# A new order for the instructions of the experts' stage, from a search with another rule for shared waits of VectorE and GpSimd

## The chip, the cores and the metric

The kernel runs on one core of a Trainium2 chip. The metric is the device time of one execution in microseconds (us), taken as the median of several runs. Five engines work side by side, each through its own queue in the order in which the program issued the instructions: TensorE (PE in the profile, with its weight loads as PEld), VectorE (DVE), ScalarE (ACT), GpSimd (POOL) and SyncE (SP), which here only starts transfers. An instruction waits on semaphores for results of other engines; whatever stands behind it in the same queue waits too.

## The reference

Two stages. Attention with packed keys: for each of 8 batches and 8 heads, `p_packed = softmax(p k^T / 8) v` with 32 packed rows, and `out = softmax(q p_packed^T / 8) p_packed`. The result is read as 4608 tokens of 512 features. Then a mixture of 8 experts with a greedy assignment:

```python
cap = N // E                       # 576 tokens for each expert
order = np.argsort(-logits.flatten())
for idx in order:                  # best pairs (token, expert) first
    tok, e = idx // E, idx % E
    if assigned[tok] >= 0 or counts[e] >= cap: continue
    assigned[tok] = e; counts[e] += 1
for e in range(E):
    mask = assigned == e
    out[mask] = np.maximum(x[mask] @ w1[e], 0.0) @ w2[e]   # 512 -> 1024 -> 512
```

## The kernel before

Attention comes first, some 140 us, in an order of its own (`ORDER`), which the change leaves alone. The experts' stage follows. For each of the 8 experts, in the order in which they fill up, three strands run at once.

The matrix work of the expert whose turn it is: every factor is split into a high and a low part, and each product is three matmuls (high by high, high by low, low by high). The hidden layer has 8 slices. For slice f, token half m and product j, `f1.k.f.m.j` is a group of four matmuls (L1390); `h_hi` (ScalarE, L1396) takes the rectified high part out of PSUM and `h_lo` (VectorE, L1401) the low part, which frees the PSUM bank. `f2.k.f.t` multiplies a slice into the output tile t (L1410 to L1412, for t = 4 L1414 and L1415). The hidden tiles and the small products of the search share three PSUM banks. At an expert's end `ev` (ScalarE) and `ev_b` (VectorE, L1433) take the outputs out, and five `scatter` transfers on GpSimd's queue (L1446, indirect) write them to the tokens' rows.

The weights of the next experts: `load` (SyncE), then `split_h` (ScalarE, L1368) makes the high part and `split_l` (GpSimd, L1374) the low part, in four instructions of a quarter each. This is the splitting that the change speaks of.

The search for later experts' tokens, mostly on VectorE: `build_a` and `build_b` (L1065, L1066) with `build_v` set up the values, eleven rounds of `count_a` (ScalarE), `count_v` (VectorE, L1104), `count_m` (TensorE, L1110, L1111) and `upd_a/b/c` (VectorE) close in on a threshold, and `slot_a` to `slot_f`, `slot_v` (two instructions, L1263), `onehot` (L1267), `list_m` (TensorE) and `list_a/s/b` turn the chosen tokens into lists. `slot_e` is L1250 to L1252. Five `gather` transfers on GpSimd's queue (L1302, indirect) fetch the rows, `xg_st` and `xg_ld` store and reload them turned, and `xt_t` (L1317), `xs_h` and `xs_l` (L1329) make the two parts of the tokens' tile.

Nothing of this order is found at run time. `PACE` is one long list of names, `step.expert.…`, that an offline search wrote, and `Later.emit` issues the steps in that order, so that each engine's queue is that list with the other engines' steps left out:

```python
def emit(self):
    order = [tuple(int(i) if i.isdigit() else i for i in k.split('.')) for k in PACE.split()]
    for k in order:
        self.ops[k][2]()
```

Times such as `LEN` and `LAND` in the file fed the search; they are not used on the chip. Waits between engines are set from what the instructions read and write.

Of the kernel before, what the change touches and what calls it, by code (L numbers as in the profile page):

```python
# [1768 lines left out]
```

## Time and profile before

| what | us |
|---|---|
| median of 3 runs | 601.55 |
| the runs | 601.39 to 603.48 |
| the profiled execution, its own time | 600.76 |
| its span, first to last instruction | 599.0 |
| TensorE busy | 580.4 (97%) |
| VectorE busy | 399.0 (67%) |
| ScalarE busy | 341.8 (57%) |
| GpSimd busy | 369.1 (62%) |

The span is what the engines' rows cover; the rest of an execution's own time lies around it. Busy time of TensorE is the union of its matmuls' spans, and a matmul's span reaches into the next one's, so a busy share tells that the queue didn't run dry, not that every start came as early as it could. The granted clock of TensorE is 0.997 of full speed over the span.

### The profile page before, as it was taken

How to read it: one execution, taken by the hardware profiler on the slowest of the kernel's cores; microseconds unless marked ns; L12 is line 12 of the kernel's file. 1: busy time of each engine (PE TensorE's matmuls, PEld its weight loads, DVE VectorE, ACT ScalarE, POOL GpSimd, SP SyncE). 2: the span in 40 equal slices, each digit the busy share in tenths (PEclk: the TensorE clock that was granted, in tenths of full speed). 3: DMA queues.
4: the chain of work that ended last, by engine and by line, in shares of the span. 5: the costliest groups of instructions: out<-in, count | busy, mean ns of one | idle time of the engine just before them, and what ended most of it. 6: DMA issues, size and time to landing. Idle time of an engine off the chain costs nothing.

```text
span 599.0 us, 12421 instructions
## 1 busy us (share of the span) xinstructions
PE 580.4 (97%) x4145; PEld 494.3 (83%) x4145; DVE 399.0 (67%) x1438; ACT 341.8 (57%) x873; POOL 369.1 (62%) x617
## 2 busy tenths in 40 slices
...
GB/s 291 391 370 261 307 333 231 192 159 225 170 10 242 123 164 208 220 91 166 249 130 113 149 242 131 150 197 182 53 203 210 239 78 196 212 8 80 1 1 84
DMA packets 75307, 105.76 MB, mean 177 GB/s; under 512 B 7124, under 2 KB 54756, under 8 KB 75236
## 3 DMA queue, kind: packets, MB, share of 16 engines
...
q8 instruction: 35, 0.57, 0.4%
q10 hardware_dynamic: 576, 0.34, 0.2%
q14 instruction: 36, 0.29, 0.2%
...
## 4 chain that ended last, share of the span: by engine, by line
PE 87%; DVE 5%; ACT 2%; POOL 2%; issue 1%; DMA 1%; SPq 0%; POOLq 0%; DVEq 0%; ACTq 0%
PE hp L1390 34%; PE y L1410 10%; PE y L1411 10%; PE y L1412 9%; PE s L530 9%; PE xp L715 4%; PE y L1414 3%; PE y L1415 2%; PE pp L589 1%; DMA kl<-in_k_dram 1%; PE tr L574 1%; PE pl L1273 1%; PE px L1335 1%; ACT ja L1098 1%; POOL sb L653 1%
## 5 line engine op out<-in xcount | busy, mean ns | idle before, releaser
L1401 DVE SCALAR_TENSOR_TENSOR h<-hp,h 128x64 fp32r<-128x64 f32 (+3 forms) x192 | 61.8, 352 | 107.4 <-ACT h L1396 106.7
L1396 ACT ACTIVATE h<-hp 128x288 fp32r<-128x288 f32 (+2 forms) x128 | 51.7, 407 | 134.0 <-PE hp L1390 65.9
L1374 POOL TENSOR_TENSOR w1l<-w1s,w1h 128x256 fp32r<-128x256 f32 x124 | 89.7, 754 | 53.4 <-ACT w1h L1368 53.2
L1374 POOL TENSOR_TENSOR w2l<-w2s,w2h 128x256 fp32r<-128x256 f32 x124 | 90.5, 761 | 47.2 <-ACT w2h L1368 47.1
L1410 PE MATMUL y<-w2h,h 128*128 128x512 f32 x256 | 103.8, 406 | 0.0
L1411 PE MATMUL y<-w2l,h 128*128 128x512 f32 x256 | 100.6, 393 | 0.0
L1412 PE MATMUL y<-w2h,h 128*128 128x512 f32 x256 | 100.2, 391 | 0.0
L1390 PE MATMUL hp<-xh,w1h 128*128 128x288 f32 (+2 forms) x512 | 89.7, 298 | 1.0 <-DVE h L1401 0.9
L1390 PE MATMUL hp<-xh,w1l 128*128 128x288 f32 (+2 forms) x512 | 90.1, 299 | 0.0
L1390 PE MATMUL hp<-xl,w1h 128*128 128x288 f32 (+2 forms) x512 | 89.8, 298 | 0.0
L1390 PEld LDWEIGHTS hp<-xh,w1h 128*128 128x128 f32 x512 | 77.8, 188 | 7.4 <-ACT h L1396 1.1
L1446 POOL DMA_INDIRECT out_dram<-xg,gi x40 | 39.3, 983 | 69.7 <-DVE xg L1433 35.7
L1098 ACT ACTIVATE ja<-Vt,nT 128x288 bf16<-128x288 f32 x116 | 62.2, 536 | 32.7 <-DVE nT L1125 24.7
L1390 PEld LDWEIGHTS hp<-xl,w1h 128*128 128x128 f32 x512 | 76.4, 188 | 3.5 <-DVE xl L1346 0.2
L1390 PEld LDWEIGHTS hp<-xh,w1l 128*128 128x128 f32 x512 | 76.0, 188 | 2.9
L1412 PEld LDWEIGHTS y<-w2h,h 128*128 128x128 f32 x256 | 48.1, 188 | 10.8
L1302 POOL DMA_INDIRECT xg<-xd,gi x40 | 38.2, 955 | 23.1 <-issue 9.2
L1410 PEld LDWEIGHTS y<-w2h,h 128*128 128x128 f32 x256 | 48.1, 188 | 4.8
L1411 PEld LDWEIGHTS y<-w2l,h 128*128 128x128 f32 x256 | 48.2, 188 | 4.5
L1116 DVE SCALAR_TENSOR_TENSOR g<-pc,thr,s4r 128x3 f32<-128x3 f32 x64 | 14.0, 219 | 41.2 <-PE pc L1111 40.9
L1368 ACT CAST w2h<-w2s 128x1024 fp32r<-128x1024 f32 x32 | 33.3, 1042 | 13.1 <-DMA w2s<-in_moe_w_dram 6.7
L715 PE MATMUL xp<-P,th 128*128 128x264 f32 (+2 forms) x160 | 38.2, 328 | 0.7 <-DVE xs L742 0.3
...
## 6 DMA issues: line engine op xcount, KB each, us to landing
...
```

What stands on the lines that cost most here:

```text
L530: nc.tensor.matmul(t[:, 224 + 9 * a:224 + 9 * b], w[:, db].rearrange("p a b -> p (a b)"), x[:, :, db, a:b].rearrange("p b (t y) -> p t b y ...
L715: nc.tensor.matmul(xp[:m, :n], T[a, g][:, o:o + m], T[w, g][:, :n], start=i == 0, stop=i == 2)
L1098: nc.scalar.activation(ja, Vf, AF.Sign, bias=S_['nT'][:, j:j + 1], scale=-1.0, accum_out=cp[:, j:j + 1])
L1302: nc.gpsimd.indirect_dma_start(out=X['xg', k, c][:m], out_offset=None, in_=xd, in_offset=bass.IndirectOffsetOnAxis(ap=X['gi', k][:m, c:c + ...
L1374: eng.tensor_sub(X[n + 'l', k, q][r], X[n + 's', k, q][r], X[n + 'h', k, q][r].bitcast(F32))
L1390: nc.tensor.matmul(X['hp', k, f, n], X[W, k, q][:, d, 128 * r:128 * r + 128], X[Z, k][:, d, cut(k) * n:576 * n + cut(k) * (1 - n)], start= ...
L1396: nc.scalar.activation(X['h', k, f][:, cut(k) * n:576 * n + cut(k) * (1 - n)], X['hp', k, f, n], AF.Relu)
L1401: V.scalar_tensor_tensor(h[:, o:o + b - a], p[:, a - t * n:b - t * n], 0.0, h[:, a:b].bitcast(F32), op0=OP.max, op1=OP.subtract)
L1410: nc.tensor.matmul(y, hh, wh, start=f == 0, stop=False)
L1411: nc.tensor.matmul(y, hh, wl, start=False, stop=False)
L1412: nc.tensor.matmul(y, hl, wh, start=False, stop=f == 7)
L1446: s = nc.gpsimd.indirect_dma_start(out=out, out_offset=bass.IndirectOffsetOnAxis(ap=X['gi', k][:m, t:t + 1], axis=0), in_=X['yo', k, t][:m ...
```

## The change

Only the list `PACE` is changed, from the middle of the search for expert 2's tokens (behind the second gather for expert 1) to the first products of expert 5; further on, only a few exchanges of near neighbours are left. Every step stays, with the same instructions and the same data: no instruction is added or removed, and each engine does the same work in another order. 428 of TensorE's 852 steps, 344 of VectorE's 626, 164 of ScalarE's 343, 58 of GpSimd's 144 and 47 of SyncE's 118 stand at another place of their queue. The search that wrote the new list went on from the old one, with a model in which every VectorE instruction that is in flight when a splitting begins behind an indirect transfer waits until the whole splitting has ended. On GpSimd's queue, 20 splittings stand directly behind a gather or a scatter before, and 18 after. Cut to the lines that the text speaks of:

```diff
@@ -125,114 +125,113 @@
...
-    upd_c.2.3 build_k.2 f1.0.6.0.2 gather.1.1 split_h.1.1.2 f1.0.6.1.1 count_m.2.3 f2.0.4.1 upd_a.2.3 h_hi.0.6.0 split_l.1.1.1 upd_b.2.3 f2.0.5.3 upd_c.2.4 count_a.2.4 h_lo.0.6.0
-    f1.0.6.1.2 count_v.2.4 f1.0.7.0.0 h_hi.0.6.1 split_h.1.2.1 count_m.2.4 f1.0.7.0.1 h_lo.0.6.1 upd_a.2.4 f1.0.7.0.2 gather.1.2 upd_b.2.4 load.1.3.1 count_v.2.5 count_a.2.5 f2.0.5.1
...
-    scatter.1.3 xs_l.2.4 f2.1.7.1 slot_d.3 ev_b.1 f1.2.0.1.0 build_a.4 scatter.1.4 f1.2.0.1.1 f1.2.0.1.2 build_b.4 f2.1.6.0 split_l.2.3.2 h_hi.2.0.1 split_h.2.3.1 slot_e.3 f2.1.7.0
-    h_lo.2.0.1 build_t.4 ev.1.1 f1.2.1.0.2 build_v.4 ev.1.0 f1.2.1.1.0 build_s.4 count_v.4.0 h_hi.2.1.0 f1.2.1.1.1 count_a.4.0 slot_f.3 scatter.1.1 load.3.1.2 f1.2.1.1.2 slot_v.3
...
-    count_v.4.1 split_h.3.0.2 h_lo.2.1.1 f1.2.2.0.1 split_l.2.3.1 list_a.3 count_m.4.1 f1.2.2.0.2 upd_a.4.1 upd_b.4.1 f1.2.2.1.0 h_hi.2.2.0 count_a.4.2 list_s.3 f2.2.0.0 list_b.3
...
-    f2.2.7.3 ev.2.1 f2.2.7.4 xs_l.3.4 ev.2.3 f1.3.0.0.0 build_b.5 ev.2.4 scatter.2.3 f1.3.0.0.1 split_h.3.3.1 ev_b.2 f1.3.0.0.2 slot_b.4 f2.2.6.2 xs_l.3.5 scatter.2.1 h_hi.3.0.0
-    build_t.5 slot_c.4 build_v.5 f2.2.7.0 slot_d.4 split_l.3.3.2 slot_e.4 f1.3.0.1.0 h_lo.3.0.0 f2.2.7.2 build_s.5 count_v.5.0 count_a.5.0 f1.3.0.1.1 build_k.5 f1.3.0.1.2 ev.2.2
...
-    upd_a.5.1 split_l.3.3.1 upd_b.5.1 list_m.4 upd_c.5.2 count_a.5.2 f2.3.0.2 count_v.5.2 list_a.4 f2.3.0.0 h_hi.3.2.0 h_lo.3.2.0 count_m.5.2 list_s.4 f2.3.1.3 upd_a.5.2 upd_b.5.2
...
-    f2.3.3.3 h_hi.3.5.0 count_a.5.10 h_lo.3.5.0 f1.3.5.1.1 count_v.5.10 f1.3.5.1.2 split_h.4.2.2 f1.3.6.0.0 count_m.5.10 f2.3.4.1 upd_a.5.10 h_hi.3.5.1 upd_c.5.10 split_l.4.2.2
...
-    xs_l.4.1 slot_d.5 f1.3.7.1.0 split_h.4.3.1 build_s.6 split_l.4.3.2 xt_t.4.3 f2.3.6.1 slot_e.5 xs_h.4.3 f1.3.7.1.1 xt_t.4.4 f1.3.7.1.2 xs_l.4.3 build_t.6 f1.4.0.0.0 h_hi.3.7.1
-    h_lo.3.7.1 split_l.4.3.1 f2.3.6.2 build_v.6 xt_t.4.5 f2.3.6.4 count_a.6.0 f2.3.6.3 count_v.6.0 f2.3.7.4 xs_h.4.4 f2.3.7.1 xs_h.4.5 ev.3.4 load.5.1.1 xs_l.4.5 f2.3.7.0 split_h.5.0.1
...
-    f2.4.4.2 h_hi.4.6.0 split_h.5.3.1 h_lo.4.6.0 slot_a.6 f2.4.5.2 xs_l.5.1 xs_l.5.0 f2.4.4.3 split_l.5.3.1 slot_b.6 test_k.7 f1.4.7.0.0 xt_t.5.2 f2.4.5.4 xt_t.5.3 slot_c.6 xs_h.5.2
...
-    xs_h.5.4 split_l.5.2.2 slot_e.6 f1.4.7.1.1 slot_f.6 f1.5.0.0.0 xt_t.5.5 f1.5.0.0.1 f1.5.0.0.2 f1.4.7.1.2 h_hi.5.0.0 load.6.0.2 f2.4.6.4 h_lo.5.0.0 h_hi.4.7.1 f2.4.6.1 onehot.6
-    xs_h.5.5 load.6.0.1 split_h.5.3.2 slot_v.6 f1.5.1.0.0 f1.5.1.0.1 xs_l.5.5 split_l.5.3.2 load.6.1.1 f2.4.6.2 h_lo.4.7.1 xs_l.5.4 f1.5.1.0.2 list_m.6 member.7 f2.4.6.0 f1.5.0.1.0
...
+    upd_c.2.3 build_k.2 f1.0.6.0.2 gather.1.1 split_h.1.1.2 f1.0.6.1.1 count_m.2.3 f2.0.4.1 upd_a.2.3 h_hi.0.6.0 gather.1.2 upd_b.2.3 f2.0.5.3 upd_c.2.4 count_a.2.4 h_lo.0.6.0
+    f1.0.6.1.2 count_v.2.4 gather.1.3 f1.0.7.0.0 h_hi.0.6.1 count_m.2.4 f2.0.4.4 upd_a.2.4 split_l.1.1.1 upd_b.2.4 f1.0.7.0.1 upd_c.2.5 count_a.2.5 f1.0.7.0.2 h_lo.0.6.1 count_v.2.5
...
+    f1.2.0.1.0 slot_d.3 h_lo.2.0.0 f1.2.0.1.1 slot_e.3 ev.1.2 build_b.4 f1.2.0.1.2 scatter.1.2 f1.2.1.0.0 slot_f.3 h_hi.2.0.1 ev.1.3 f1.2.1.0.1 h_lo.2.0.1 split_h.3.0.1 onehot.3
+    build_t.4 f1.2.1.0.2 scatter.1.3 build_v.4 f1.2.1.1.0 h_hi.2.1.0 build_s.4 ev_b.1 f1.2.1.1.1 count_a.4.0 count_v.4.0 f1.2.1.1.2 scatter.1.4 h_lo.2.1.0 f2.2.0.2 h_hi.2.1.1 slot_v.3
+    count_m.4.0 f1.2.2.0.0 split_l.2.3.2 upd_a.4.0 h_lo.2.1.1 f1.2.2.0.1 upd_b.4.0 f1.2.2.0.2 list_m.3 h_hi.2.2.0 count_a.4.1 f1.2.2.1.0 h_lo.2.2.0 list_a.3 f1.2.2.1.1 upd_c.4.1
+    split_l.2.3.1 load.3.1.2 f1.2.2.1.2 count_v.4.1 list_s.3 h_hi.2.2.1 count_m.4.1 f2.2.0.1 upd_a.4.1 upd_b.4.1 list_b.3 f1.2.3.0.0 count_a.4.2 upd_c.4.2 f2.2.0.4 count_v.4.2
...
+    xs_h.3.2 h_lo.2.6.1 slot_a.4 f2.2.5.4 xs_l.3.2 f1.2.7.0.1 xs_l.3.1 f1.2.7.0.2 close_b.5 f1.2.7.1.0 h_hi.2.7.0 f1.2.7.1.1 h_lo.2.7.0 build_a.5 f2.2.6.1 f2.2.5.2 slot_b.4 build_b.5
+    split_h.3.3.2 f2.2.6.3 xt_t.3.3 build_t.5 slot_c.4 split_h.3.3.1 split_l.3.3.2 f1.2.7.1.2 build_s.5 build_v.5 f2.2.6.2 count_v.5.0 h_hi.2.7.1 xs_h.3.3 slot_d.4 f1.3.0.0.0
+    h_lo.2.7.1 count_a.5.0 xt_t.3.4 f2.2.6.0 f1.3.0.0.1 xs_l.3.3 load.4.1.2 f1.3.0.0.2 xt_t.3.5 f2.2.6.4 h_hi.3.0.0 count_m.5.0 xs_h.3.4 f2.2.7.4 upd_a.5.0 slot_e.4 xs_h.3.5 f2.2.7.3
...
+    list_a.4 f1.3.2.0.0 upd_b.5.2 upd_c.5.3 count_a.5.3 f1.3.2.0.1 count_v.5.3 split_l.3.3.1 f1.3.2.0.2 list_s.4 h_hi.3.2.0 f2.3.1.3 split_h.4.0.2 count_m.5.3 f2.3.0.4 upd_a.5.3
...
+    xs_h.4.2 split_h.4.3.1 build_a.6 slot_a.5 f2.3.5.3 split_h.4.2.2 f1.3.7.0.2 xs_l.4.2 f1.3.7.1.0 build_b.6 h_hi.3.7.0 split_l.4.2.2 f2.3.5.0 slot_b.5 build_s.6 h_lo.3.7.0 f1.3.7.1.1
+    xt_t.4.3 build_t.6 f1.4.0.0.0 build_v.6 xs_h.4.3 f1.3.7.1.2 xt_t.4.4 split_h.4.3.2 f2.3.6.0 xs_l.4.3 split_l.4.3.1 f1.4.0.0.1 h_hi.3.7.1 xs_h.4.4 h_lo.3.7.1 f2.3.6.1 count_a.6.0
+    count_v.6.0 f1.4.0.0.2 xt_t.4.5 f2.3.7.0 h_hi.4.0.0 xs_h.4.5 h_lo.4.0.0 split_l.4.3.2 count_m.6.0 slot_c.5 load.5.1.1 upd_a.6.0 f2.3.6.3 slot_d.5 upd_b.6.0 load.5.0.2 count_v.6.1
...
+    f1.4.6.1.0 xs_l.5.0 f1.4.6.1.1 xs_h.5.1 split_l.5.2.2 f1.4.7.0.0 xt_t.5.2 f1.4.7.0.1 xs_l.5.1 f1.4.6.1.2 f1.4.7.0.2 f2.4.5.3 h_hi.4.7.0 load.6.0.2 xs_h.5.2 h_lo.4.7.0 f2.4.5.4
...
+    h_hi.4.7.1 split_l.5.3.2 f1.5.1.0.1 h_lo.4.7.1 f2.4.6.2 xs_l.5.4 xs_l.5.5 f1.5.1.0.2 f2.4.6.4 member.7 list_m.6 split_l.5.3.1 f2.4.6.0 load.6.1.2 f1.5.0.1.0 h_hi.5.1.0
```

## Rows read from the trace of the kernel before

**Rows 1.** stretches of the run: span, its length, busy us (instructions) by engine, clock, DMA
```profile
196.00:266.00 70.00, 70.00 (x454) 59.67 (x453) 51.24 (x250) 46.66 (x117) 43.76 (x63) 1.00 0.53 159
266.00:276.00 10.00, 9.02 (x55) 7.60 (x55) 9.58 (x26) 5.63 (x13) 8.72 (x13) 1.00 0.61 197
276.00:320.00 44.00, 44.00 (x284) 38.36 (x284) 31.71 (x146) 25.66 (x65) 25.21 (x34) 1.00 0.60 174
320.00:336.00 16.00, 15.16 (x110) 13.23 (x109) 13.19 (x48) 9.39 (x24) 11.48 (x17) 1.00 0.29 107
336.00:445.00 109.00, 109.00 (x697) 95.96 (x696) 74.25 (x321) 61.52 (x146) 67.39 (x96) 1.00 0.56 166
452.00:590.60 138.60, 138.60 (x824) 124.71 (x822) 40.59 (x98) 43.44 (x82) 63.25 (x94) 1.00 0.38 114
590.60:599.00 8.40, 0.00 (x0) 0.00 (x0) 0.49 (x2) 0.37 (x1) 1.46 (x3) 0.80 0.26 88
```

**Rows 2.** every wait of TensorE for another engine from 150 to 598 us
```profile
PE hp L1390 <- DVE h L1401: 0.9, 1, 0.9
PE pc L1110 <- ACT ja L1098: 0.7, 1, 0.7
```

**Rows 3.** timeline of TensorE, 266 to 275 us
```profile
270.91 0.77 PE L1390 MATMUL hp<-xh,w1l 128*128 128x288 f32 x4
272.60 0.77 PE L1390 MATMUL hp<-xh,w1h 128*128 128x288 f32 x4 [0.92 <-DVE h L1401]
```

**Rows 4.** timeline of VectorE, 266 to 275 us
```profile
268.33 1.42 DVE L1065 TENSOR_SCALAR wm<-eq 128x288 f32<-128x288 f32 x1
269.78 0.88 DVE L1066 TENSOR_TENSOR wm<-wm,Lw 128x288 f32<-128x288 f32 x1
270.59 0.70 DVE L1250 TENSOR_SCALAR s2i<-sl 128x36 int32<-128x36 int32 x1
...
273.90 0.90 DVE L1263 TENSOR_TENSOR Bv<-hr,pv 128x648 bf16<-128x648 bf16 x2
```

**Rows 5.** timeline of TensorE, 321 to 335 us
```profile
325.73 0.70 PE L1390 MATMUL hp<-xh,w1l 128*128 128x288 f32 x4
326.26 0.69 PE L1390 MATMUL hp<-xh,w1h 128*128 128x288 f32 x4
327.62 0.16 PE L1110 MATMUL pc<-cp,same 128*128 128x3 f16 x1 [0.67 <-ACT ja L1098]
...
328.28 0.69 PE L1390 MATMUL hp<-xh,w1l 128*128 128x288 f32 x4
329.04 0.77 PE L1390 MATMUL hp<-xh,w1h 128*128 128x288 f32 x4
```

**Rows 6.** timeline of VectorE, 321 to 335 us
```profile
323.68 0.61 DVE L1250 TENSOR_SCALAR s2i<-sl 128x36 int32<-128x36 int32 x1
324.21 0.78 DVE L1251 TENSOR_SCALAR s2i<-sl 128x36 int32<-128x36 int32 x1
325.02 0.68 DVE L1252 CAST sbf<-s2i 128x72 bf16<-128x72 int32 x1
```

**Rows 7.** timeline of GpSimd, 266 to 337 us
```profile
268.75 3.22 POOL L1374 TENSOR_TENSOR w2l<-w2s,w2h 128x256 fp32r<-128x256 f32 x4
...
276.01 3.37 POOL L1374 TENSOR_TENSOR w1l<-w1s,w1h 128x256 fp32r<-128x256 f32 x4
...
323.50 2.81 POOL L1374 TENSOR_TENSOR w2l<-w2s,w2h 128x256 fp32r<-128x256 f32 x4
```

**Rows 8.** timeline of GpSimd, 440 to 453 us
```profile
447.41 2.81 POOL L1374 TENSOR_TENSOR w1l<-w1s,w1h 128x256 fp32r<-128x256 f32 x4
```

**Rows 9.** timeline of VectorE, 444 to 453 us
```profile
446.91 3.94 DVE L1267 TENSOR_TENSOR A<-sbf,iob 128x1152 bf16<-128x1152 bf16 x1
```

**Rows 10.** the instructions of L1065: count, shortest/median/longest ns
```profile
L1065 DVE TENSOR_SCALAR wm<-eq x6: 300/307/1417, 145.2 to 369.7; 128x288 f32<-128x288 f32 x6
```

**Rows 11.** the instructions of L1267: count, shortest/median/longest ns
```profile
L1267 DVE TENSOR_TENSOR A<-sbf,iob x8: 748/753/3943, 136.8 to 446.9; 128x1152 bf16<-128x1152 bf16 x8
```

More of the change, by code (lines that the diff above doesn't have):

```diff
@@ L187 @@
-    load.5.1.2 count_m.6.0 f1.4.0.0.1 upd_a.6.0 upd_b.6.0 ev.3.0 f1.4.0.1.0 xs_l.4.4 f1.4.0.0.2 ev_b.3 scatter.3.0 f1.4.0.1.1 upd_c.6.1 h_hi.4.0.0 slot_f.5 count_a.6.1 f2.3.7.3
-    scatter.3.4 h_lo.4.0.0 f1.4.0.1.2 count_v.6.1 ev.3.3 f1.4.1.0.0 h_hi.4.0.1 count_m.6.1 scatter.3.3 f2.3.7.2 ev.3.1 upd_a.6.1 h_lo.4.0.1 f1.4.1.0.1 slot_v.5 ev.3.2 f1.4.1.0.2
-    scatter.3.1 upd_b.6.1 onehot.5 f1.4.1.1.0 count_a.6.2 f1.4.1.1.1 scatter.3.2 list_m.5 h_hi.4.1.0 f1.4.1.1.2 h_lo.4.1.0 split_l.5.0.1 upd_c.6.2 f2.4.0.4 h_hi.4.1.1 list_a.5
@@ new lines @@
+    scatter.0.2 test_t.2 close_b.3 f1.1.2.0.2 h_lo.1.1.1 slot_a.2 f2.1.0.0 h_hi.1.2.0 load.2.0.2 slot_b.2 build_a.3 scatter.0.3 slot_c.2 load.2.1.1 f2.1.0.4 slot_d.2 f1.1.2.1.0
+    slot_e.2 f1.1.2.1.1 slot_f.2 f1.1.2.1.2 build_b.3 f2.1.0.3 h_hi.1.2.1 slot_v.2 split_h.1.3.2 f2.1.0.1 build_s.3 onehot.2 build_t.3 split_h.2.0.1 f2.1.1.4 split_l.1.3.2 build_v.3
+    f2.1.1.3 h_lo.1.2.1 count_a.3.0 count_v.3.0 list_m.2 h_lo.1.2.0 f1.1.3.1.0 list_a.2 count_m.3.0 f2.1.0.2 upd_a.3.0 upd_b.3.0 load.2.1.2 list_s.2 upd_c.3.1 count_a.3.1 f1.1.3.1.1
@@ new lines @@
+    split_l.3.2.1 upd_a.4.9 load.3.3.1 upd_b.4.9 h_hi.2.5.0 f2.2.4.3 count_v.4.10 count_a.4.10 h_lo.2.5.0 f1.2.5.1.2 f1.2.6.0.0 h_hi.2.5.1 count_m.4.10 f1.2.6.0.1 upd_a.4.10 upd_c.4.10
+    split_l.3.2.2 f2.2.4.1 upd_b.4.10 h_lo.2.5.1 bound_m.4 f1.2.6.0.2 bound_a.4 test_c.4 f1.2.6.1.0 h_hi.2.6.0 test_m.4 h_lo.2.6.0 f1.2.6.1.1 test_k.4 f2.2.5.1 xt_t.3.0 f2.2.5.3
+    xt_t.3.1 xs_h.3.0 f2.2.4.0 bound.4 test_t.4 xs_h.3.1 assign.4 f2.2.4.4 xs_l.3.0 f1.2.7.0.0 member.4 expert.4 xt_t.3.2 f1.2.6.1.2 load.4.0.2 f2.2.5.0 h_hi.2.6.1 close_a.5 load.4.0.1
@@ new lines @@
+    upd_b.5.0 xs_l.3.5 count_a.5.1 f2.2.7.2 xs_l.3.4 f1.3.0.1.0 h_lo.3.0.0 upd_c.5.1 ev.2.2 f1.3.0.1.1 slot_f.4 ev.2.4 f1.3.0.1.2 count_v.5.1 ev.2.3 f2.2.7.1 slot_v.4 h_hi.3.0.1
+    scatter.2.3 count_m.5.1 f2.2.7.0 upd_a.5.1 h_lo.3.0.1 f1.3.1.0.0 upd_b.5.1 build_k.5 ev.2.0 scatter.2.2 f1.3.1.0.1 count_a.5.2 f1.3.1.0.2 count_v.5.2 scatter.2.0 f1.3.1.1.0
+    onehot.4 h_hi.3.1.0 f1.3.1.1.1 ev.2.1 h_lo.3.1.0 f1.3.1.1.2 ev_b.2 scatter.2.1 count_m.5.2 list_m.4 upd_c.5.2 h_hi.3.1.1 split_h.4.0.1 f2.3.0.3 h_lo.3.1.1 scatter.2.4 upd_a.5.2
```

174 lines of the change are left out of this document (83 added, 91 removed).

## The prediction

> **What bounds the kernel now.** I read four views in this order. First the busy time by stretches, to find where TensorE stands still. From 196 to 266 us, 276 to 320, 336 to 445 and 452 to 590.6 its busy time equals the stretch; only 266 to 276 (9.02 of 10) and 320 to 336 (15.16 of 16) fall short, by 0.98 and 0.84 us, and the last 8.40 us are the end, without matmuls [rows 1]. So the experts' stage is TensorE's own work, back to back, with two holes. Second the list of TensorE's waits: from 150 to 598 us it waited for another engine twice, 0.9 us for `h_lo` on VectorE and 0.7 us for `count_a` on ScalarE [rows 2]. Third the timelines around the two, to size them by starts, since a matmul's span runs into the next. A group of four at full rate starts 0.53 us after the one before (325.73, 326.26) [rows 5]. The first hole: a group at 270.91, so the next was due at 271.44 and came at 272.60: 1.16 us lost [rows 3]. The second: due at 326.79, came at 327.62: 0.83; and behind it one due at 328.81 came at 329.04: 0.23 [rows 5]. **2.22 us in all**: this is the most that a new order of the same steps can give back, because the matrix work itself stays, and the end is issued in nearly the same order.
>
> Fourth, why VectorE was late there. At 268.33 a `build_b` instruction took 1.42 us [rows 4], where the median of its line is 0.307 [rows 10]: 1.11 too long. GpSimd's splitting had begun at 268.75, inside it [rows 7]. The next two took 0.88 and 0.70 [rows 4], and the `h_lo` that frees TensorE's bank stands behind them. At 323.50 a splitting began [rows 7], and the three `slot_e` instructions in it took 0.61, 0.78 and 0.68, 2.07 together for tiles of 36 and 72 columns [rows 6]; `count_a` waits behind them. So both holes come from VectorE's waits while GpSimd splits, and both splittings follow a scatter. The reader is to see that a much longer wait cost nothing: `onehot` at 446.91 took 3.94 us [rows 9] where its median is 0.753 [rows 11], 3.19 too long, and ended only after the whole splitting of 447.41 to 450.22 [rows 8], yet TensorE has no wait there [rows 2].
>
> **The change part by part.** Nothing is added or removed, so each cost is one of place.
>
> Moved out, expert 3: `build_b.4` and `slot_e.3` stood around `split_l.2.3.2`, which follows `scatter.1.4`. In the new list both come before `scatter.1.2`, and so do not meet it; `onehot.3` also stands ahead of it, and `split_l.2.3.1` follows the other splitting directly. Value: the first hole, 1.16.
>
> Moved out, expert 4: `split_l.3.3.2` stood behind `scatter.2.1` and next to `slot_e.4`. Now it follows `split_l.3.2.2`, earlier, and between it and `slot_e.4` stand f1.2.7.1.2, f1.3.0.0.0, f1.3.0.0.1 and f1.3.0.0.2 besides f2 groups. The four f1 groups are 4 x 0.53 = 2.1 us; f2.2.6.2 and f2.2.6.0 are three matmuls of 512 columns each, more columns than an f1 group's four of 288, so at least 1.1 us more. That is 3.2 us, and the splitting of 2.81 us [rows 7] is over first. Value: 0.83 and 0.23, 1.06.
>
> Moved in, the one place with a contending instruction behind a transfer: `split_l.2.3.2` still follows `scatter.1.4`, with `slot_v.3` just ahead of it. Below: nothing, if `slot_v` is through, or is held for a short time; above: the whole-splitting price of `onehot`, 3.19. What hides it: on TensorE `count_m.4.0` and three f1 groups stand between `slot_v.3` and `list_m.3`, which needs it, 3 x 0.53 = 1.59 us with `count_m` at nothing. `slot_v` takes 0.90 for both its instructions [rows 4]. So the cover beyond it is 0.69, and the price on TensorE runs from 0 to 3.19 - 0.69 = 2.50; late next would be `upd_a.4.0` and `h_lo.2.1.1`, queued behind it on VectorE. Three starts behind a scatter show what happens: at 447.41 an instruction waited for all of the splitting [rows 8, 9]; at 268.75 one ended at 269.75, with the splitting lasting to 271.97 [rows 4, 7]; at 276.01 it was the splitting that stretched, to 3.37 us against 2.81 [rows 7]. Two of three are short, so I take nothing here by itself, and a share of the allowance below.
>
> [...]
>
> Moved in, plain splittings: `build_b.6` and `xs_l` stand next to `split_l.4.2.2` and `split_l.4.3.1`, `slot_v.6` next to `split_l.5.3.2`. They follow splittings, which the search's model leaves without a wait. Price from 0 (VectorE has cover, as at 447) to that of the second hole, 1.06, at each of two changes of expert.
>
> Moves of loads, stores and gathers on SyncE and GpSimd's queue (47 and 58 places): I take nothing. TensorE waited for no transfer in this stage [rows 2], and in the new list 16 to 18 f1 and f2 groups stand between an expert's last reload (`xg_ld`) and its first `xt_t`, as 17 to 20 did before. Without that cover the cost would be the lateness itself.
>
> The sum: -1.16 - 1.06 = -2.22 returned. The old list was left with three losses, of 0.74 on average; new places are untried, so I allow one of that size for all the places above: +0.74. Net -1.48. The profiled execution would go from 600.76 to 599.3 (span 599.0 to 597.5), and the median, 0.79 above it, from 601.55 to **600.1 us**.
>
> **The rivals.** *A (`slot_v` waits for the whole splitting).* For it: 3.94 us at 446.91 [rows 9]; against: the shorter ones [rows 4]. It decides once the wait passes 0.69 us. 601.55 - 2.22 + 2.50 = 601.8.
>
> *B (the change guards the wrong moment).* VectorE waits in any splitting, whenever its instruction begins, and the list has moved contending work to plain ones. For it: the `slot_e` instruction at 323.68 began inside the splitting, not before it [rows 6, 7], and was held all the same. Against it: 3.19 us of waiting cost nothing where VectorE had time [rows 2, 9]. Two changes of expert at 1.06 each: 601.55 - 2.22 + 2.12 = 601.5, as if nothing had been done. [...]
>
> *C (slower).* Waits for the whole splitting are the usual thing in the new order, at the changes to experts 3, 4 and 5, where VectorE is nearly full (9.58 of 10 in the first hole [rows 1]). One costs 2.50 uncovered; two leave 601.55 - 2.22 + 5.00 = 604.3, so it decides at the third: 606.8. Against it: the one such wait seen cost nothing.
>
> *D (more is returned than I can see),* under 598.5: TensorE's busy stretches [rows 1] speak against it.
>
> **How the numbers follow.** The measurement of this kernel tells a change from none at about 0.5%, 3.0 us: 598.5 to 604.6. Forecast 0.57, A 0.13, B 0.16, C 0.08, D 0.06. The forecast's own range is 598.9 to 601.0: all 2.22 back with the runs' spread on the low side (0.16, and as much again on the other comparison), to half of it back. The range is **598.9 to 602.6**: the upper end is A with the one extra loss, 601.8 + 0.74. It leaves out C and D and a little of B. Faster by over 0.5% comes from D alone, 0.06; slower from C, 0.08; within it the forecast, A and B, 0.86.
>
> **What would show it.** Right: in the new trace TensorE's waits of 0.9 for `h_lo` and 0.7 for `count_a` are gone, `build_b.4` takes about 0.3, each `slot_e` instruction about 0.2 to 0.4, and the last matmul ends 1 to 2 us earlier, near 589. A shows as an L1263 instruction of over 2 us near 273 and a wait of TensorE for it at L1273. B shows as L1065, L1263 or L1329 rows of 0.6 to 1.4 us inside plain splittings, with TensorE waiting for `h_lo` near 365 to 375 or 425 to 435. C shows as several instructions of over 2 us, with VectorE's busy time above 399.0 by as much. I am wrong altogether if TensorE waits at a place that has nothing to do with splitting: at an expert's first product for its tokens, or for weights.

## The result, and the profile after

The changed kernel takes **607.84 us** (median of six runs, 604.97 to 608.96) where the kernel before took 602.18 beside it: a ratio of 1.008, with a 95% interval of 1.0057 to 1.0103. It is slower by 0.8%, outside the range of the prediction and on the side to which it gave 0.08. The profiled execution took 608.3 us, with a span of 606.5.

TensorE's waits behind the attention show where. These are all from 150 to 606 us (line, what it waited for, us in total, times, longest); they answer to [rows 2], and every line number behind `PACE` is one less than before:

```profile
PE pl L1272 <- DVE g L1115: 4.5, 1, 4.5
PE pc L1109 <- ACT ja L1097: 2.0, 2, 1.6
```

Neither of the old waits is there; one of 4.5 us at `list_m` is. By starts it cost more. TensorE's timeline of the changed kernel:

```profile
277.30 0.69 PE L1389 MATMUL hp<-xh,w1l 128*128 128x288 f32 x4
282.51 1.24 PE L1272 MATMUL pl<-Bv,A 128*128 128x144 bf16 x9 [4.53 <-DVE g L1115]
283.49 1.31 PE L1389 MATMUL hp<-xh,w1h 128*128 128x288 f32 x4
284.60 1.16 PE L1389 MATMUL hp<-xl,w1h 128*128 128x288 f32 x4
285.56 1.16 PE L1389 MATMUL hp<-xh,w1l 128*128 128x288 f32 x4
286.52 0.43 PE L1284 MATMUL plw<-ld,rep 128*128 128x18 bf16 x8
...
299.45 1.22 PE L1389 MATMUL hp<-xh,w1l 128*128 128x288 f32 x8
302.30 0.16 PE L1109 MATMUL pc<-cp,same 128*128 128x3 f16 x1 [1.63 <-ACT ja L1097]
```

A group of four began at 277.30, the next work was due 0.53 us later [rows 5], at 277.83, and came at 282.51: **4.68 us** lost, here called the gap. Behind it the starts from 283.49 on are 1.11, 0.96 and 0.96 us apart, where a group of four takes 0.53 at full rate. The windows of the changed kernel say why (columns as in [rows 1]: the stretch, its length, the busy time of TensorE, its weight loads, VectorE, ScalarE and GpSimd, then the granted clock and the DMA's share and rate):

```profile
7.28:14.10 6.82, 6.82 (x27) 5.93 (x26) 3.99 (x8) 1.90 (x6) 1.82 (x22) 0.50 1.06 322
266.00:276.00 10.00, 10.00 (x66) 8.89 (x64) 8.98 (x31) 7.78 (x16) 5.14 (x9) 1.00 0.43 162
276.00:320.00 44.00, 37.85 (x240) 33.16 (x239) 31.37 (x128) 20.46 (x56) 27.04 (x38) 0.92 0.56 156
320.00:336.00 16.00, 16.00 (x97) 13.51 (x96) 14.87 (x53) 9.54 (x22) 3.70 (x6) 1.00 0.31 99
280.34:287.17 6.83, 4.66 (x32) 4.51 (x32) 4.28 (x16) 1.67 (x5) 1.22 (x2) 0.50 0.43 143
```

The stretch 266 to 276 is now full (10.00 of 10, before 9.02) and so is 320 to 336 (16.00 of 16, before 15.16): both old holes are closed. From 276 to 320, which was full before, 6.15 us are missing. And from 280.34 to 287.17 the granted clock is 0.50, where it was 1.00 from 266 to 276: TensorE had been without work for 2.5 us when it fell (277.83 to 280.34), and ran at half for 4.7 us more when its work came (282.51 to 287.17).

What held it is on VectorE. Its timeline, and GpSimd's, of the changed kernel:

```profile
270.63 0.17 DVE L1249 TENSOR_SCALAR s2i<-sl 128x36 int32<-128x36 int32 x1
271.04 0.30 DVE L1064 TENSOR_SCALAR wm<-eq 128x288 f32<-128x288 f32 x1
...
275.57 6.75 DVE L1262 TENSOR_TENSOR Bv<-hr,pv 128x648 bf16<-128x648 bf16 x2
282.25 0.20 DVE L1115 SCALAR_TENSOR_TENSOR g<-pc,thr,s4r 128x3 f32<-128x3 f32 x1
...
296.55 3.41 DVE L1069 TENSOR_TENSOR ck<-eq,k 128x288 f32<-128x288 f32 x1
```

```profile
275.12 0.90 POOL L1445 DMA_INDIRECT out_dram<-xg,gi  x1 [0.34 <-DVE xg L1432]
276.05 2.79 POOL L1373 TENSOR_TENSOR w2l<-w2s,w2h 128x256 fp32r<-128x256 f32 x4
278.81 2.75 POOL L1373 TENSOR_TENSOR w1l<-w1s,w1h 128x256 fp32r<-128x256 f32 x4
...
294.06 2.82 POOL L1373 TENSOR_TENSOR w2l<-w2s,w2h 128x256 fp32r<-128x256 f32 x4
296.84 2.80 POOL L1373 TENSOR_TENSOR w1l<-w1s,w1h 128x256 fp32r<-128x256 f32 x4
```

What the change moved out does well: `build_b.4` takes 0.30 us (1.42 in [rows 4]) and `slot_e.3` 0.17 (0.70 there). But `slot_v.3`, 0.90 us in [rows 4], takes **6.75**. It began at 275.57; the splitting behind `scatter.1.4` began at 276.05; and a second splitting follows it without a pause, where the old order had three scatters between the two. `slot_v` ended at 282.32, after both were over at 281.56 (278.81 and 2.75), and `upd_a.4.0`, for which `list_m` waited by the list above, stood behind it. The same thing at 296.55, smaller: `build_k.4` (median 0.456 us on this line) took 3.41, to the end of a plain splitting that began inside it, `count_a` came late, and TensorE, due at 300.51 behind eight matmuls (2 x 0.53), went on at 302.30: 1.79 us lost.

One part of the 608.3 is not the change's. The profiled run had its clock at half from 7.28 to 14.10 us, at the start of the attention, in code that is the same in both; the experts' first splitting began at 158.44 us, 2.6 later than before. About half of the profiles below show such a start (kernel 4, for one, from 7.65 to 14.47 us) and half do not, whatever was altered. So the profiles are compared below by **the stretch from the experts' first splitting to the end of the last matmul**: 434.72 us before (155.88 to 590.60), 440.10 after (158.44 to 598.54). The difference of 5.38 fits that of the medians, 5.66.

### The profile page after: what moved, and what is told of

It reads as the page before. It is cut to its first block, busy times and chain, and to the rows that moved or that the text cites. A ratio compares the mean times of both kernels' runs of the same rounds, so it can differ in the third digit from the quotient of the medians.

```text
span 606.5 us, 12424 instructions
## 1 busy us (share of the span) xinstructions
PE 583.8 (96%) x4143; PEld 498.3 (82%) x4145; DVE 400.8 (66%) x1438; ACT 341.7 (56%) x873; POOL 367.8 (61%) x617
## 4 chain that ended last, share of the span: by engine, by line
PE 88%; DVE 5%; POOL 3%; ACT 2%; issue 1%; DMA 1%; SPq 0%; POOLq 0%; DVEq 0%; ACTq 0%
PE hp L1389 33%; PE y L1409 10%; PE y L1410 10%; PE y L1411 10%; PE s L529 9%; PE xp L714 4%; PE y L1413 3%; PE y L1414 2%; PE pp L588 1%; DVE Bv L1262 1%; PE tr L573 1%; PE pl L1272 1%; PE s L538 1%; PE px L1334 1%; DMA w2s<-in_moe_w_dram 1%
```

## The experiments

Each takes the changed kernel and alters what is shown. Diffs are of the order on one engine's queue, cut to the place. In the table, stretch is the one just defined; `slot_v` is the longer of `slot_v.3`'s two instructions; gap is what TensorE lost there, by starts as above; half clock is the time of granted clock 0.5 that followed. Stretch, `slot_v`, gap and half clock are of one profiled execution of each kernel.

| kernel | median us | ratio to before, 95% | stretch | `slot_v` | gap | half clock |
|---|---|---|---|---|---|---|
| changed | 607.84 | 1.0057 to 1.0103 | 440.10 | 6.34 | 4.68 | 280.34 to 287.17 |
| 1 `slot_v` early | 600.39 | 0.9953 to 0.9984 | 432.04 | 0.48 | none | no |
| 2 splittings parted | 601.76 | 0.9984 to 1.0022 | 433.58 | 3.62 | 1.96 | no |
| 3 `build_k` away | 608.46 | 1.0097 to 1.0139 | 439.15 | 6.35 | 4.68 | 279.73 to 286.56 |
| 4 both of 1 and 3 | 601.31 | 0.9970 to 1.0006 | 432.62 | 0.48 | none | no |
| 5 memset before each | 606.37 | 1.0035 to 1.0095 | 438.61 | 6.56 | 4.90 | 280.81 to 287.63 |
| 6 one memset between | 606.60 | 1.0054 to 1.0100 | 438.33 | 6.38 | 4.71 | 280.55 to 287.38 |
| 7 run of three | 609.70 | 1.0075 to 1.0171 | 441.06 | 9.06 | 7.40 | 283.00 to 289.82 |
| 8 gap filled | 604.39 | 1.0010 to 1.0063 | 436.28 | 6.36 | 0.4 | no |

**1 and 15. `slot_v` early.** The step is moved past two others, so that it is over before the splitting begins.

```diff
  VectorE
   ev_b.1
+  slot_v.3
   count_v.4.0 h_lo.2.1.0
-  slot_v.3
   upd_a.4.0 h_lo.2.1.1
```

> The changed kernel with one step moved on VectorE: slot_v.3 ahead of count_v.4.0 and h_lo.2.1.0, so that it runs while scatter.1.4 is in flight and is over before split_l.2.3.2 begins. Theory (the 0.8% is mostly one wait: slot_v.3 in flight when the splitting began, held until both splittings of the run were over, and TensorE's slower clock behind it): slot_v back to about 0.9 us for both, TensorE's gap at list_m gone (4.7 us), its clock at full rate through 270 to 300 (about 2 us more): 607.8 - 6.7 = about 601 us, the second hole near 300 us (1.8 us) staying. Rival 1 (the clock's fall has another cause than the gap): only the gap comes back, about 603 us, granted clock still at half for a stretch near 280. Rival 2 (whichever VectorE instruction is in flight then is held): the next one behind, upd_a.4.0 or h_lo.2.1.1, takes over 2 us near 276 and the time stays at 605 to 608 us.

Measured 600.39 us. A row of VectorE's timeline of this kernel, and one of GpSimd's:

```profile
276.36 0.88 DVE L1262 TENSOR_TENSOR Bv<-hr,pv 128x648 bf16<-128x648 bf16 x2
```

```profile
277.64 2.79 POOL L1373 TENSOR_TENSOR w2l<-w2s,w2h 128x256 fp32r<-128x256 f32 x4
```

`slot_v` is back at 0.88 us for both and ends at 277.24, before the splitting at 277.64. TensorE then waits for no other engine from 160 us to its last matmul, and its clock is 1.00 from 16 to 596 us. The stretch is 8.06 us shorter than the changed kernel's. With this one step moved the whole loss is gone. The second hole is gone too, which the expectation left standing: `build_k`, at 291.85, took 0.88 us and not 3.41. Why is not shown, for here too a splitting began inside it, at 292.29; this time the splitting gave way, and took 3.12 us. The first theory stands, both rivals fall. The same kernel on another occasion:

> The version with slot_v.3 ahead of count_v.4.0 once more, beside the one with drains on the same chip. If the gain of 0.3% over the kernel before is the order's and not the chip's, its ratio is again 0.995 to 0.999.

600.51 us beside 603.07, 0.9943 to 0.9987: again some 0.3% below the kernel before. Its stretch is 432.02 us, where the first profile had 432.04.

**2. The splittings parted.** `slot_v` stays in harm's way; the second splitting is moved behind a gather.

```diff
  GpSimd
   scatter.1.4 split_l.2.3.2
-  split_l.2.3.1
   gather.3.3
+  split_l.2.3.1
   gather.3.2 gather.3.4 gather.3.0 gather.3.1
```

> The changed kernel with one step moved on GpSimd: split_l.2.3.1 behind gather.3.3, so that split_l.2.3.2 is no longer followed directly by another splitting; slot_v.3 stays where it was, in flight when split_l.2.3.2 begins. Theory (VectorE is let go when GpSimd's unbroken run of splitting instructions ends): slot_v is held for one splitting, about 2.8 us beyond its own time instead of 5.9, TensorE's gap at list_m falls from 4.7 to about 2 us: 603 us if the clock then stays at full rate, 605 us if it falls all the same. Rival 1 (the length of the wait is set by something else than GpSimd's run): slot_v again over 6 us, 607 to 608 us. Rival 2 (the moved splitting and the gathers behind it hold up something later): slot_v short, but a new wait for a gather or for w1l.

Rows of the timelines of GpSimd, VectorE and TensorE of this kernel:

```profile
274.56 2.79 POOL L1373 TENSOR_TENSOR w2l<-w2s,w2h 128x256 fp32r<-128x256 f32 x4
283.03 2.81 POOL L1373 TENSOR_TENSOR w1l<-w1s,w1h 128x256 fp32r<-128x256 f32 x4
```

```profile
274.09 4.03 DVE L1262 TENSOR_TENSOR Bv<-hr,pv 128x648 bf16<-128x648 bf16 x2
```

```profile
275.82 0.69 PE L1389 MATMUL hp<-xh,w1l 128*128 128x288 f32 x4
278.31 0.72 PE L1272 MATMUL pl<-Bv,A 128*128 128x144 bf16 x9 [1.80 <-DVE g L1115]
```

`slot_v` ended at 278.12 with the one splitting (277.35) behind it, the gap is 1.96 us, the clock did not fall, and the median is 601.76, below the 603 expected (`build_k` took 0.80 us here). The wait ended with GpSimd's unbroken run, now of one splitting.

**3. `build_k` away.** The other held step, moved to where GpSimd splits nothing.

```diff
  VectorE
   upd_b.4.2
+  build_k.4
   h_lo.2.2.1 ... count_v.4.5 upd_c.4.5
-  build_k.4
```

> The changed kernel with one step moved on VectorE: build_k.4 behind upd_b.4.2, about 8 us earlier, where GpSimd issues gathers and splits nothing. Theory (the second hole is build_k.4 held for a whole plain splitting): build_k back to 0.46 us, TensorE's wait for count_m near 302 us (1.8 us lost) gone, slot_v's long wait unchanged: about 606 us. Rival (TensorE's loss there is the slow stretch's aftermath, VectorE being behind anyway): the loss near 300 us stays or moves to the next count_m, 607 to 608 us.

`build_k` takes at most 0.454 us here, so its wait is gone; but TensorE now waits 0.5 us for `count_v` near 291 us, and the stretch is 0.95 us shorter, not 1.79. The median of 608.46, of four runs, shows no gain where about 606 us was expected: a miss in time, though the held step was let go.

**4. Both moves,** those of 1 and 3 together.

> The changed kernel with both moves on VectorE: slot_v.3 ahead of count_v.4.0, build_k.4 behind upd_b.4.2. Theory (two held instructions and the clock behind the first are the whole of the loss): 607.8 - 6.7 - 1.8 = about 599.3 us, 2 us below the kernel before, whose own two holes of 2.2 us the new order has not. Rival (the new order has other losses, that the profile of one run hides): 602 us or more, no better than the kernel before.

601.31 us, not 599.3, and not better than experiment 1. Moved to its new place `build_k` makes `count_v` late: TensorE waits 0.45 us for it at 286.24. In experiment 1, where it stayed, it cost nothing.

**5 and 6. Something between the subtractions.** A GpSimd memset of one element ahead of each of the seven later subtractions of the two splittings (5), or only between the two splittings (6).

```diff
     kernel 5, in split_l
-        for r in (slice(None),) if eng is V else quarters(which):
+        for j, r in enumerate((slice(None),) if eng is V else quarters(which)):
+            if j + 3 * (which == 1) and (k, q) == (2, 3):
+                nc.gpsimd.memset(spc, 0.0)
     kernel 6, in split_l
+        if (k, q, which) == (2, 3, 1):
+            nc.gpsimd.memset(spc, 0.0)
         for r in (slice(None),) if eng is V else quarters(which):
```

> The changed kernel with a GpSimd memset of one element ahead of each of the seven later instructions of split_l.2.3.2 and split_l.2.3.1, so that no two subtractions stand directly behind each other there; the order is unchanged. Theory 1 (VectorE is let in only where GpSimd's queue has no next instruction ready, whatever its kind): slot_v held as before, over 6 us, 607 to 608 us, a little more for the memsets. Theory 2 (VectorE is let in wherever a subtraction is not followed directly by the next one): slot_v held for one subtraction, about 0.7 us beyond its 0.49, TensorE's gap at list_m nearly gone, about 601 us. If the memsets themselves take VectorE's place, the wait lies between.

> The changed kernel with one GpSimd memset of one element between split_l.2.3.2 and split_l.2.3.1; the order is unchanged. Theory 1 (only an empty queue lets VectorE in): slot_v over 6 us, 607 to 608 us. Theory 2 (a break between two subtractions lets it in): slot_v about 3.6 us as with the two splittings parted, TensorE's gap about 2 us, its clock kept, 602 us.

Rows of the timelines of GpSimd and VectorE of the kernel with one memset (6):

```profile
276.31 2.79 POOL L1375 TENSOR_TENSOR w2l<-w2s,w2h 128x256 fp32r<-128x256 f32 x4
279.04 0.09 POOL L1373 MEMSET spc<- 1x1 f32 x1
279.09 2.75 POOL L1375 TENSOR_TENSOR w1l<-w1s,w1h 128x256 fp32r<-128x256 f32 x4
```

```profile
275.82 6.78 DVE L1262 TENSOR_TENSOR Bv<-hr,pv 128x648 bf16<-128x648 bf16 x2
```

In both `slot_v` waits as before. The memset begins 0.06 us before the last subtraction ends, and the next subtraction 0.04 us before the memset does; GpSimd never stands still. Another instruction between, without a pause, did not part the run. Both kernels are shorter in the stretch than the changed one, by 1.5 and 1.8 us: in their profiles `build_k` was not held (0.77 us at most in the kernel with one memset). That prices the second hole anew: 440.10 - 438.33 = 1.77 us, where the starts had 1.79.

**7. A run of three.**

```diff
  GpSimd
   split_l.2.3.2 split_l.2.3.1
+  split_l.3.0.2
   gather.3.3 ... gather.3.1
-  split_l.3.0.2
```

> The changed kernel with split_l.3.0.2 moved ahead of the gathers of expert 3, directly behind split_l.2.3.1: an unbroken run of three splittings, 8.4 us, with slot_v.3 in flight as it begins. Theory (held for the whole run): slot_v 6.35 + 2.8 = about 9.1 us, TensorE's gap at list_m 4.7 + 2.8 = 7.5 us, the gathers 2.8 us later: 610 to 612 us. Rival (the wait has a length of its own, or ends with the second splitting): slot_v at 6.3 us, 606 to 608 us, since one later splitting of expert 3 is out of the way.

The timelines of GpSimd and VectorE of this kernel, the run and the row held:

```profile
275.88 2.79 POOL L1373 TENSOR_TENSOR w2l<-w2s,w2h 128x256 fp32r<-128x256 f32 x4
278.64 2.75 POOL L1373 TENSOR_TENSOR w1l<-w1s,w1h 128x256 fp32r<-128x256 f32 x4
281.37 2.75 POOL L1373 TENSOR_TENSOR w2l<-w2s,w2h 128x256 fp32r<-128x256 f32 x4
```

```profile
275.41 9.06 DVE L1262 TENSOR_TENSOR Bv<-hr,pv 128x648 bf16<-128x648 bf16 x1
```

The first `slot_v` instruction took 9.06 us and the gap was 7.40, each 2.72 more than in the changed kernel, as the theory has it. The stretch grew by only 0.96, since `build_k` was not held here (0.62 us): 2.72 - 1.77 = 0.95. The median, 609.70, is just under the 610 to 612 expected.

**8. The gap filled.** `slot_v` is held as before; TensorE gets 20 products of the zero tile that serve nothing.

```diff
     def list_m():
+        if ('hp', 2, 2, 0) in X and ('y', 2, 3) not in X:
+            X['y', 2, 3] = PL['ps'].tile([128, 512], F32, name="y3")
+            keep_warm(nc, X['y', 2, 3], wz, 20)
         p = S_['pl'] = bank("pl")
```

> The changed kernel with 20 products of the zero tile that serve nothing (128 x 512, bf16, into y3's bank before its first real product) ahead of list_m.3 on TensorE, to fill the gap of 4.7 us there; slot_v is held as before. Theory (the gap's idleness is what takes the clock to half, and that costs about 2 us behind it): granted clock at full rate through 280 to 288, the groups of first products behind list_m 0.53 us apart instead of 0.96 to 1.11, 607.8 - 2 = about 605.8 us. Rival (the clock falls for another reason): half rate for a stretch near 280 all the same, 607 to 608 us. If the products outlast the gap, they add what they overrun, below 0.5 us.

TensorE's timeline of this kernel, and one of its windows (the clock is the third number from the end):

```profile
278.88 4.26 PE L415 MATMUL y<-wz 128*128 128x512 bf16 x19
283.36 0.72 PE L1275 MATMUL pl<-Bv,A 128*128 128x144 bf16 x9 [0.21 <-DVE g L1115]
283.88 0.78 PE L1392 MATMUL hp<-xh,w1h 128*128 128x288 f32 x4
284.50 0.70 PE L1392 MATMUL hp<-xl,w1h 128*128 128x288 f32 x4
```

```profile
280.00:284.00 4.00, 3.79 (x25) 1.98 (x24) 4.00 (x9) 0.04 (x1) 2.40 (x4) 1.00 0.41 140
```

The clock stays at 1.00 and the groups behind `list_m` begin 0.62 us apart. `build_k` is not held here, so the right comparison is experiment 6, where the gap is empty and it is not held either: 438.33 - 436.28 = **2.05 us is what the slow clock costs**. With the same wait, work that serves nothing made the kernel faster: 604.39 us, where kernel 6 took 606.60 on the same occasion.

**9 to 12. When the instruction begins.** Two theories are set against each other: that whatever is in flight waits, and that only a narrow moment is bad. A VectorE memset of one element ahead of `slot_v` (9), three (10), `slot_v` behind `h_lo.2.1.1` (11), `slot_v` and `h_lo.2.1.0` exchanged (12).

```diff
     kernels 9 and 10, in slot_v of expert 3, once or three times
+            V.memset(tny, 0.0)
     kernel 11, VectorE
   h_lo.2.1.0
-  slot_v.3
   upd_a.4.0 h_lo.2.1.1
+  slot_v.3
     kernel 12, VectorE
   count_v.4.0
+  slot_v.3
   h_lo.2.1.0
-  slot_v.3
```

> The changed kernel with one VectorE memset of a single element ahead of slot_v.3: slot_v begins about 0.1 us later, so 0.3 to 0.4 us ahead of split_l.2.3.2 instead of 0.48, and is still in flight when that begins. Theory 1, the model behind the change (whatever VectorE instruction is in flight when a splitting follows a transfer waits for the whole run): slot_v over 6 us as before, 606 to 608 us. Theory 2 (the long wait comes only where the instruction begins in a narrow moment ahead of the splitting, 0.48 to 0.50 us in all long waits behind a transfer so far, while those of 0.36, 0.38 and 0.59 us were short): the first subtraction stretches to about 1.0 to 1.3 us, slot_v takes 0.3 to 0.6 us more and TensorE's gap is below 0.8 us: 600 to 602 us.

> The same with three such memsets: slot_v begins 0.1 to 0.3 us ahead of the splitting. Theory 1: over 6 us, 606 to 608 us. Theory 2: short waits, 600 to 602 us; if the first slot_v instruction begins about 0.3 us ahead, where one long wait behind another splitting was seen (build_k at 296.55), it may be held all the same.

> The changed kernel with slot_v.3 behind h_lo.2.1.1 on VectorE, so that it begins inside the run of two splittings and not ahead of it. Theory 1 as the change has it (only what is in flight at the start waits): no long wait, slot_v a few tenths late, list_m about 1 us late for its later place: 601 to 603 us. [...]

> The changed kernel with slot_v.3 and h_lo.2.1.0 exchanged on VectorE: slot_v's first instruction is over before the splitting, its second begins about 0.44 us ahead and would end with the splitting's start. Theory 1: the second instruction waits for the whole run, 6 us, and h_lo.2.1.0 behind it too: 607 us or more. Theory 2 (narrow moment): no long wait, about 601 us, unless 0.44 us is still inside the moment, which then is wider than 0.48 to 0.50.

| kernel | `slot_v` began, to the run's start | `slot_v` | TensorE's gap | median us | ratio, 95% |
|---|---|---|---|---|---|
| 9 | 0.47 ahead | 6.33 | 4.69 | 605.65 | 1.0034 to 1.0090 |
| 10 | 0.23 ahead | 6.09 | 4.69 | 605.30 | 1.0044 to 1.0098 |
| 11 | 0.87 inside | 5.00 | 4.55 | 608.52 | 1.0069 to 1.0143 |
| 12 | 0.45 ahead | 6.27 | 6.14 | 608.84 | 1.0072 to 1.0132 |

The narrow moment falls. (In 9 the single memset shifted nothing; `slot_v` began as before.) So does the model that the change was searched with. Rows of the timelines of VectorE and GpSimd of kernel 11:

```profile
278.35 0.52 DVE L1400 SCALAR_TENSOR_TENSOR h<-hp,h 128x224 fp32r<-128x224 f32 x2
278.79 5.41 DVE L1262 TENSOR_TENSOR Bv<-hr,pv 128x648 bf16<-128x648 bf16 x2
```

```profile
277.92 2.79 POOL L1373 TENSOR_TENSOR w2l<-w2s,w2h 128x256 fp32r<-128x256 f32 x4
280.68 2.75 POOL L1373 TENSOR_TENSOR w1l<-w1s,w1h 128x256 fp32r<-128x256 f32 x4
```

Here `slot_v` was not in flight when the run began: it began at 278.79, inside it, and waited for the end at 283.43 all the same. And the two `h_lo` instructions just ahead of it ran through, 0.52 us together, in the middle of the same run. In 12 the longer wait comes from the queue: `h_lo.2.1.0` stands behind the held `slot_v`, and TensorE waits 6.0 us for the bank that it frees.

The medians of 9 and 10 lie 2.2 and 2.5 us below that of the changed kernel, with the same gap. In the profile of 10 `build_k` was not held (0.69 us) and the half clock lasted 3.41 us; in that of 9 both were as in the changed kernel. Whether `build_k` is held in some executions of one kernel and not in others is not shown.

In kernel 12 the clock fell behind a gap of 1.92 us too. `build_k` was held there (3.55 us), and behind it TensorE, due at 300.88, went on at 302.80. Rows of its timeline and one of its windows:

```profile
299.82 1.22 PE L1389 MATMUL hp<-xh,w1l 128*128 128x288 f32 x8
302.80 0.16 PE L1109 MATMUL pc<-cp,same 128*128 128x3 f16 x1 [1.76 <-ACT ja L1097]
```

```profile
303.20:306.40 3.20, 3.20 (x9) 2.51 (x8) 1.99 (x12) 2.33 (x6) 0.07 (x1) 0.50 1.12 247
```

Behind this gap of 1.92 us the granted clock was 0.50, from 303.12 to 306.54; behind the 1.96 us of kernel 2 and the 1.79 of the changed kernel it stayed at 1.00.

**13, 14, 16. A real pause.** Not a memset but a drain, at which GpSimd's timeline of kernel 13 shows it standing still, some 0.16 us or longer: ahead of the seven later subtractions of the two splittings (13, and again as 16), and in all splittings of experts 1 to 7 (14).

```diff
     kernels 13 and 16, in split_l, j counting the quarters
+            if j + 3 * (which == 1) and (k, q) == (2, 3):
+                nc.gpsimd.drain()
     kernel 14
+            if (j or which == 1) and k and eng is not V:
+                nc.gpsimd.drain()
```

> The changed kernel with a GpSimd drain (wait until its own instruction before is done) ahead of each of the seven later subtractions of split_l.2.3.2 and split_l.2.3.1; the order is unchanged, slot_v.3 in flight as before. Theory (VectorE gets in only when GpSimd has nothing running for a moment; consecutive subtractions overlap by about 0.05 us, so it never has inside a run): with the overlap gone slot_v waits for one subtraction, 0.5 to 0.8 us beyond its 0.49, TensorE's gap at list_m is under 1 us, its clock stays: 601 to 602 us. [...]

> The changed kernel with such a drain between the subtractions of every splitting of experts 1 to 7, and between splittings. Theory: no VectorE instruction waits longer than one subtraction anywhere (onehot near 455 us 1.5 us or less instead of 3.94, build_k near 297 us 1.1 us or less), TensorE without a gap over 1 us: 600 to 602 us, unless the splittings, longer by the drains, make a first product late. Rival: long waits as before, 606 to 608 us.

> The version with drains in the two splittings once more, beside the one with slot_v.3 early. If its ratio of 0.989 came from the chip, on which the kernel before took 614 us, it is here 0.997 to 1.003, a little above the version with slot_v.3 early, since slot_v still waits about 1 us. If the drains themselves bring something, it is again below 0.992 and below that version's.

Rows of the timelines of GpSimd and VectorE of kernel 13:

```profile
276.75 0.75 POOL L1375 TENSOR_TENSOR w2l<-w2s,w2h 128x256 fp32r<-128x256 f32 x1
279.79 2.50 POOL L1375 TENSOR_TENSOR w2l<-w2s,w2h 128x256 fp32r<-128x256 f32 x3 [2.29 <-issue]
282.44 0.74 POOL L1375 TENSOR_TENSOR w1l<-w1s,w1h 128x256 fp32r<-128x256 f32 x1 [0.16 <-issue]
```

```profile
276.27 1.99 DVE L1262 TENSOR_TENSOR Bv<-hr,pv 128x648 bf16<-128x648 bf16 x2
```

`slot_v` takes 1.59 us at most: one subtraction, 276.75 to 277.50, and then its own time. With a pause it gets in. The pause that let it in was the long one: GpSimd stands 2.29 us at the first drain, which comes behind a scatter (1.26 in 14), and some 0.16 at each later one. Two rows of VectorE's timeline of 14 are the nearest that the runs come to the short pauses:

```profile
222.53 1.02 DVE L1256 TENSOR_TENSOR hr<-sbf,i 128x648 bf16<-128x648 bf16 x1
224.35 1.02 DVE L1065 TENSOR_TENSOR wm<-wm,Lw 128x288 f32<-128x288 f32 x1
```

Each began inside a subtraction and ran behind it, across a pause of 0.16 us, but neither stands at a place where a long wait was seen. On the chip of 13 and 14 the kernel before took 614.27 us; 13 took 607.37 (0.9845 to 0.9928) and 14 took 623.44 (1.0108 to 1.0199). In 14 `onehot`, 3.94 us at its longest before [rows 9] and in the changed kernel, takes 0.764 at most; but there it was over, at 460.48, while GpSimd still issued a scatter, so that this says nothing of pauses. TensorE waits 5.9 us for one late `h_lo` and 8.7 for eight `count_a`: as a cure it is worse than the ill. Kernel 16, which is 13 again on a chip where the kernel before took 603.07, took 604.39 (0.9987 to 1.0049), against 600.51 for that of experiment 1: the 0.989 did not come back on another chip, and beside the kernel before the drains bring nothing. The gap at `list_m` is gone in both, but TensorE waits for late `count_a` elsewhere, 4.9 us in six places in 13 and 2.8 us in one in 16, with the clock at half from 308.48 to 311.89 behind it: stretches of 440.39 and 436.07 us, and the 601 to 602 us expected were not reached.

## Why the prediction was wrong

**What was right.** The two holes were where [rows 2] has them, both are closed, and closing them is worth at least what the sum says: with `slot_v` out of the way (experiment 1) the stretch is 2.68 us below that of the kernel before, and 2.70 in the second profile, where the prediction had 2.22 as the most; where the rest comes from is not shown. The median of 600.39 lies by the forecast's 600.1. In the changed kernel itself three of the four signs of being right are there (both waits gone, `build_b.4` and `slot_e` short); the fourth, the last matmul near 589 us, is not: it ended at 598.54. The moves of loads, stores and gathers cost nothing, as assumed: no wait of TensorE in the changed kernel is for a transfer. The `xl` and `slot_v.6` instructions moved next to plain splittings cost nothing either; of 36 `xl` instructions the longest took 1.09 us, and TensorE has no wait from 320 us to its last matmul.

**The step that failed** is "Moved in, the one place with a contending instruction behind a transfer". It named the place, the instruction, `list_m` and `upd_a.4.0` behind it, and then took nothing for it, with 2.50 as the upper bound. Measured: 4.68 us of gap and about 2 us of slow clock behind it. Three things were off. *The value taken:* two of three waits in the old trace were short, but of eleven kernels here with `slot_v` in that place or near it, and no pause in GpSimd's run, none has a short one. *The bound:* it used the price of one splitting, 3.19 [rows 9, 11], though the paragraph on expert 3 just ahead of it says that `split_l.2.3.1` now follows directly; a run of two holds for 5.86 (6.34 less its own 0.48), of three for 8.58. The cover that it counted, 0.69, was in fact 5.86 - 4.68 = 1.18. *The wake:* nothing in the sum allowed for TensorE's clock falling in a gap. No gap of the experts' stage in the old trace was longer than 1.16 us; but the last line of [rows 1], without matmuls, has the clock at 0.80: there too it was lower while TensorE stood.

Rival A was this wait, at this place and with this sign in the trace (an instruction of over 2 us on the line now numbered 1262, TensorE waiting at `list_m`); its time of 601.8 was too low by the same terms. Rival C came out on the right side and near the time (606.8) by luck, by another route: three uncovered waits at three changes of expert, where there were two at one. Its sign, VectorE's busy time above 399.0 by as much as the waits, did not show: it was 400.8, with 5.86 and 2.95 us of waiting. The bounds of the forecast's own range do not come out of their working either: 601.55 - 2.22 with two times 0.16 is 599.0 and not 598.9, and half of 2.22 back is 600.4 and not 601.0; nothing hangs on it.

**A step that was not there:** `build_k.4`, moved to the second of a pair of splittings, 1.79 us. The prediction listed `build_b.6`, `xs_l` and `slot_v.6` for plain splittings and missed it. In the old order it ran inside another splitting, at 303.37, and took 0.95 us. Rival B is half right: the wait needs no transfer ahead of the splitting; but its places, near 365 to 375 and 425 to 435 us, show no wait.

The sum by what was measured: the order without `slot_v`'s wait gives -2.68 against the kernel before; +4.68 for the gap, +1.79 for `build_k`, +2.05 for the clock; together +5.84, where the stretch grew by 5.38.

**Which instructions waited.** Two lines of the changed kernel, `h_lo` and `xl` (count, shortest/median/longest ns):

```profile
L1400 DVE SCALAR_TENSOR_TENSOR h<-hp,h x192: 202/391/460, 154.8 to 589.8; 128x64 fp32r<-128x64 f32 x64, 128x288 fp32r<-128x288 f32 x56, 128x224 fp32r<-128x224 f32 x56, 128x256 fp32r<-128x256 f32 x16
```

```profile
L1328 DVE TENSOR_TENSOR xl<-xt,xh x36: 510/552/1093, 257.9 to 546.7; 128x384 fp32r<-128x384 f32 x36
```

`h_lo`, which reads one input from a PSUM bank, took 0.46 us at most in 192 instructions, and kernel 11 shows two of them in the middle of a run, 0.52 us together, while `slot_v` just behind them, which reads nothing from such a bank, took 5.00 us. Whether the bank is the reason is not shown. Beginning first did not spare an instruction the wait: `slot_v` began 0.48 us ahead of the splitting in the changed kernel, and still waited for all eight subtractions, 5.86 us, and not for one of 0.70 (a quarter of 2.79). In the kernel before, too, the `build_b` instruction that began 0.42 us ahead of a splitting lost more than one subtraction: 1.11 us [rows 4, 7, 10].

**Left open:** why `xl`, which reads nothing from a PSUM bank either, was let in (at 381.92 us, inside a run of three splittings from 378.91 to 388.04, one took 1.01 us, where the median of its line is 0.55), and why `build_k` at the same place was held for a whole splitting in the changed kernel, while in kernel 6 the splitting gave way to it instead (3.10 us against 2.80). How far ahead it began does not tell: it was held at 0.29, 0.31 and 0.41 us (changed, 9, 12) and let in at 0.24 to 0.44 (1, 2, 5, 6, 8, 10, 11). No run here separates type, shape or a finer phase. The long waits that were seen ended where GpSimd's run ended or paused.
